# The first chunk of a fused mLSTM and MLP kernel: up-projection blocks in quarters, clearings on ScalarE, a new order of conversions

## The chip, the cores and the metric

The kernel runs on one core of a Trainium2 chip. The metric is device time in microseconds: 498.03 us, the median of 13 runs (496.6 to 499.7). The core has five engines that run their own instruction queues in order and meet at semaphores: TensorE (matrix products, PE in the profile, its weight loads PEld), VectorE (DVE), ScalarE (ACT), GpSimd (POOL) and SyncE (SP), which here issues all DMA transfers.

## The reference

Two stages. The first is an mLSTM cell: for 4 batches x 8 heads, head size 40, over 768 time steps, a matrix memory is decayed, added to and read out.

```python
for t in range(S):
    kt, vt, qt = (k[:, :, t], v[:, :, t], q[:, :, t])
    m_new = np.maximum(f_gate[:, :, t] + m, i_gate[:, :, t])
    f_stab = np.exp(f_gate[:, :, t] + m - m_new)
    i_stab = np.exp(i_gate[:, :, t] - m_new)
    m = m_new
    C = f_stab[:, :, None, None] * C + i_stab[:, :, None, None] * np.einsum('bhd,bhe->bhde', vt, kt)
    n = f_stab[:, :, None] * n + i_stab[:, :, None] * kt
    h_tilde = np.einsum('bhde,bhe->bhd', C, qt)
    nq = np.einsum('bhd,bhd->bh', n, qt)[:, :, None]
    denom = np.maximum(np.abs(nq), 1.0)
    o = 1.0 / (1.0 + np.exp(-o_gate[:, :, t]))
    y[:, :, t] = o * h_tilde / denom
```

Its output, as 3072 tokens x 320, feeds the second stage, with w_in 320 x 2048 and w_out 2048 x 320. All arrays but the two weight matrices are float32; those two are float64.

```python
h = x @ w_in
g = h * (1.0 / (1.0 + np.exp(-1.702 * h)))
return (g @ w_out).astype(np.float32)
```

## The kernel before

**Chunks.** The 768 steps are cut into six chunks of 128 (`w` = 0 to 5). A chunk's attention is computed as within-chunk products plus what the carried state gives. Each chunk then goes through the MLP: an up part of eight blocks `j` with two output tiles of 128 hidden units x 512 tokens (4 batches x 128), and a down part in which the attention of the next chunk is interleaved. The order of all instructions is written out by hand: each engine runs its share in program order.

**The attention steps of chunk 0**, one batch `b` at a time:

- `transposes(0, b)` (L297) transposes keys and queries by TensorE and copies them out of PSUM by ScalarE (L310).
- `weights(0, b)` (L319) builds the exponents of the decay weights by small bf16 products (L324, L328, L329) from `pick`, `m3` and `a3`, in two halves, and ScalarE takes their exponential (L330). `m3` comes from VectorE and `a3` from GpSimd, both in `gates(0)` (L239), which starts with a scan over the gates (L244).
- `scores(0, b)` (L341) multiplies keys and queries; VectorE multiplies the result into the weights (L349).
- `values(0, b)` (L351) multiplies weights and values; VectorE divides and applies the output gate (L383 to L389), and GpSimd copies 64 columns of y (L391). With `states=True` it also emits `scale_values` (L402), in which GpSimd multiplies the values by their decay for the state.
- `seam(0, b)` (L393) transposes y by TensorE into `p_x`, and ScalarE copies it to `xT` (L399), the input of the MLP.
- `gate_out(b)` (L684) is ScalarE's tanh of the output gate. `columns(0)` (L283) brings per-step factors into columns.

**PSUM.** There are three rings of banks: `ps_a` with four tiles, used in turn by every attention step (a new tile waits until the readers of the tile four places before it are done), `ps_m` with two and `ps_x` with two, which hold the up blocks' sums. `keep_busy(n)` (L183) issues `n` bf16 products of zeros (128 x 512); nobody reads them. Before the change they all go to one tile of `ps_m`.

**Weights.** A float64 weight is loaded as two 32-bit words and turned into a float32 by `convert(n)` (L222), in pieces of 128 x 512: two ScalarE instructions ("A", L227 and L228) and then four VectorE ones ("V", L231 to L236). Pieces 0, 1, 3, 4, 5, 6, 8 and 9 are rows 0 to 255 of w_in: blocks 0 and 1 need pieces 0 and 1, blocks 2 and 3 need 3 and 4, blocks 4 and 5 need 5 and 6, blocks 6 and 7 need 8 and 9. Pieces 2 and 7 hold rows 256 to 319, for blocks 0 to 3 and 4 to 7. Pieces 10 to 19 are w_out. `fetch(n)` (L156) issues a piece's loads on SP, into a slot that an earlier piece must have left.

**The up part of chunk 0.** `up(w, j, n)` (L447) computes `n` blocks. A block is `full` (two 128-row parts of w_in, for both tiles) and `rest` (the last 64 rows), then the GELU by ScalarE (L474). For blocks 0 and 1, `full` is done for the first 256 tokens (batches 0 and 1), then a function `between` is called, then the other 256 tokens follow. That function is `rest_of_first` (L732): values, seams and conversions of batches 2 and 3. `weights_in(n)` (L744) calls `convert` and then `fetch` for the pieces in a table: `weights_in(0)` converts piece 5 and fetches 10 to 15.

**Clearings.** Early in the kernel, GpSimd clears the padding of the key and query buffers, `k_bl` (128 x 2048, L203) and, later, `state` (128 x 1312, L710).

The calls that set the order of chunk 0, from L700 to L730, and the functions that the diff touches:

Of the kernel before, what the change touches and what calls it, by code (L numbers as in the profile page):

```python
# [8 lines left out]
FP = mybir.dt.float32  # L9
U32 = mybir.dt.uint32  # L10
BF = mybir.dt.bfloat16
AF = mybir.ActivationFunctionType
# [10 lines left out]
L = 128  # L23
# [11 lines left out]
def kernel(  # L35
# [22 lines left out]
    W = B * L  # L58
# [118 lines left out]


    idle = const.tile([128, 128], BF, name="idle")
    V.memset(idle, 0.0)  # L180
    p_idle = ps_m.tile([128, W], FP, tag="m", name="p_idle")

    def keep_busy(n):  # L183
        for _ in range(n):
            T.matmul(p_idle, idle, idle.unsqueeze(1).to_broadcast([128, 4, 128]), start=True, stop=True)

    keep_busy(8)
    ident = const.tile([128, 128], FP, name="ident")
    make_identity(nc, ident)
    one1 = const.tile([BH, 1], FP, name="one1")  # L190
# [9 lines left out]
    for t in (k_st, q_st):  # L200
        G.memset(t[:, :, D:DP], 0.0)
    G.memset(v_st[:, :, D:D1], 1.0)
    G.memset(k_bl, 0.0)  # L203

    not_yet, ident_bf = (xs.bitcast(BF)[:, i * L:(i + 1) * L] for i in range(2))
    V.memset(not_yet, 0.0)
    G.affine_select(out=not_yet, in_=not_yet, compare_op=OP.is_ge, fill=NEG, base=0, pattern=[[1, L]],
                    channel_multiplier=-1)
    V.tensor_copy(out=ident_bf, in_=ident)
# [1 line left out]
    a3 = const.tile([3 * BH, L], BF, name="a3")  # L211
    m3 = const.tile([3 * BH, L], BF, name="m3")
    state = const.tile([128, BH // 2, 2, D1], FP, name="state")

    t1, t2, t4 = (const.tile([128, NH, DH], FP, name=f"t{i}") for i in (1, 2, 4))

# [124 lines left out]
    def scores(w, b):  # L341
        pool, tag = (ps_x, "x") if w > 1 and b % 2 == 0 else (ps_a, "a")
        pw = [pool.tile([L, NP, L], FP, tag=tag, name="p_s") for _ in range(2)]
        for p in range(NP):
            for i in range(2):
                r = slice(i * 64, i * 64 + D)
                T.matmul(pw[i][:, p, :], kT[w, b][r, p, :], qT[w, b][r, p, :], start=True, stop=True)
        for i in range(2):
            V.tensor_tensor(out=wt[w, b][:, :, i, :], in0=pw[i], in1=wt[w, b][:, :, i, :], op=OP.mult)  # L349
# [43 lines left out]
    def seam(w, b):  # L393
        if b == 0:
            xT[w] = work.tile([128, 3, B, L], FP, tag="xT", bufs=1, name="xT")
        px = ps_a.tile([128, 3, L], FP, tag="a", name="p_x")
        for c in range(3):
            T.transpose(px[:, c, :], ys[w, b][:, c * 128:(c + 1) * 128], ident)  # L398
        A.copy(out=xT[w][:, :, b, :], in_=px)  # L399
# [44 lines left out]

    w_half = [[w_in_sb[:, c, :].rearrange("p (n h m) -> h p n m", h=2, m=256)[i] for c in range(2)] for i in range(2)]

    def up(w, j, n, between=None, states=False):  # L447

        x = xT[w].rearrange("p c b t -> p c (b t)")
        begin, end = range(j, j + n // 2), range(j + n // 2, j + n)
        ph = {}

        def take(j, pool, tag):
            ph[j] = [pool.tile([128, W], FP, tag=tag, name="p_h") for _ in range(2)]

        def full(j, first, ts=slice(0, W)):
            for c in range(2):  # L460
                for i in range(2):
                    T.matmul(ph[j][i][:, ts], w_half[i][c][:, j // 2, j % 2 * 128:(j % 2 + 1) * 128], x[:, c, ts],  # L462
                             start=(first and c == 0 and ts.start == 0), stop=(not first and c == 1),
                             skip_group_check=between is not None)

        def rest(j, first):
            for i in range(2):
                r = slice(i * 64, i * 64 + 64)
                T.matmul(ph[j][i], w_in_x[r, j, :], x[r, 2, :], start=first, stop=not first,
                         skip_group_check=between is not None)  # L470

        def gelu(j):
            for i, g in enumerate(hidden_of(w, j)):
                A.activation(out=g, in_=ph[j][i], func=AF.Gelu_apprx_sigmoid)  # L474

        if between:
            begin, end = (j, j + 1), ()
        for k in begin:
            take(k, *((ps_m, "m") if k == j else (ps_x, "x")))
            full(k, True, slice(0, W // 2 if between else W))  # L480
        if between:
            between()
            for k in begin:
                full(k, True, slice(W // 2, W))
        if states:
            new_states(w)
            carry(w)
        for k in begin:
            rest(k, False)
            gelu(k)  # L490
        for k in end:
            if k not in ph:
                take(k, *((ps_x, "x") if n == 2 else (ps_a, "a")))
            rest(k, True)
        for k in end:
            full(k, False)
            gelu(k)
# [209 lines left out]
    gate_out(0)  # L707
    gate_out(1)
    values(0, 0)
    G.memset(state, 0.0)  # L710
    convert(0, "A")
    values(0, 1)
    keep_busy(2)
    seam(0, 0)
    transposes(0, 2)
    convert(0, "V")
    seam(0, 1)
    convert(1, "A")
    weights(0, 2)
    keep_busy(2)  # L720
    transposes(0, 3)
    weights(0, 3)
    convert(1, "V")
    columns(0)
# [2 lines left out]
    scale(0, 0)  # L727
    scale(0, 1)
    scores(0, 2)
    scores(0, 3)  # L730

    def rest_of_first():  # L732
        values(0, 2, 3, states=True)
        seam(0, 2)
        seam(0, 3)
        for n in (2, 3, 4):
            convert(n)

# [15 lines left out]
    for w in range(NW):  # L756
        more = w + 1 < NW
        for j in range(NF // 2):
            if j % 2 == 0:
                if w:  # L760
                    if j % 4 == 0:
                        if w > 1:
                            up_fast(w, j, next_keys if more and j == 0 else None)
                        else:
                            up(w, j, 4, states=(j == 0))
                elif j == 0:
                    up(w, j, 2, rest_of_first)
                    weights_in(0)
                else:
                    weights_in(j // 2)  # L770
                    up(w, j, 2, states=(j == 2))
            if j == 0 and more:
                load(w + 1, "o")
            if w == 0 and j == 0:
                load_blocks(1, 0)
                spread(1)
            if w == 1 and j == 1:
                weight_sums()
                first_sums()
            if more:  # L780
                if w == 1 and j == 0:
                    gates(w + 1)
                if j == 4:
                    if w == 0:
                        load_blocks(1, 1)
                    load(w + 1, "v")
                    if w:
                        spread(w + 1)
                if j == (4 if w else 6):
                    load(w + 1, "k")  # L790
                if w == 1 and 4 <= j < 6:
                    transposes(w + 1, 2 * j - 8)
                    transposes(w + 1, 2 * j - 7)
            if w > 1 and more and j == 3:
                transposes(w + 1, 2)
                transposes(w + 1, 3)
            if w and j in (3, 7):
                hidden_sums(w, 0, (j // 4 * 2, j // 4 * 2 + 1), 1, 2)
                if j == 3:
                    hidden_sums(w, 0, (0, 1), 3, 4)  # L800
        side = attention(w + 1) if more else []
        if w == 0:

            blocks = [(lambda b=b, n=n: down(w, b, n)) for ns in ((0, 1), (2,), (3,)) for b in range(B) for n in ns]
            stops = (0, 1, 5, 7, 9, 11, 13, 15)
        else:
            blocks = down_fast(w, 0) + down_fast(w, 1)
            stops = (0, 1, 2, 4, 8, 10, 11, 12)
        for i, block in enumerate(blocks):
            if w == 0:  # L810
                weights_in(4 + i)
                for b in {2: (0, 1), 7: (2,), 9: (3,)}.get(i, ()):
                    transposes(1, b)
            elif w + 2 < NW and i == 0:
                load_gates(w + 2)
                load_blocks(w + 2)
            block()
            if i in stops and side:
                run(side.pop(0))
            if w:  # L820
                for at, c, *what in ((0, 0, (2, 3), 3), (1, 0, (2, 3), 4), (1, 1, range(4), 1),
                                     (5, 1, range(2), 2), (6, 1, range(2, 4), 2), (7, 1, range(4), 4)):
                    if i == at:
                        hidden_sums(w, c, *what)
                if i == 2 and not more:
                    hidden_sums(w, 1, range(4), 3)
            if w == 1 and i == 9:
                first_difference()
        if w == 0:
            load_gates(2)  # L830
            load_blocks(2)
# [30 lines left out]
```

## Time and profile before

| | us |
|---|---|
| median of 13 runs | 498.03 |
| lowest and highest run | 496.6, 499.7 |
| the profiled execution | 496.6 |
| its span, first to last instruction | 494.9 |
| TensorE busy | 484.4 |
| VectorE busy | 330.7 |
| ScalarE busy | 207.3 |
| GpSimd busy | 63.1 |

The profile describes one execution. Its page gives the busy time of each engine, then the span in 40 equal slices of 12.4 us, each digit the busy share in tenths, and the clock granted to TensorE in tenths of full speed. Queries of the same trace give the list of waits (who waited for whom), the timeline (start and length of instructions, merged where alike, with the idle time before them in brackets and what ended it), and busy times in chosen stretches. A float32 product appears as two instructions for one matmul of the program. DMA issues have a time from issue to landing. A matmul's end is modelled, so products that follow each other closely overlap in the rows.

### The profile page before, as it was taken

What the parts mean: (1) busy time and instruction counts of PE and PEld (TensorE: products, weight loads), DVE (VectorE), ACT (ScalarE), POOL (GpSimd) and SP (SyncE); (2) the same over time, 40 slices, a digit from 0 to 9 for tenths busy, and PEclk for the clock granted to TensorE, in tenths of its full rate; (3) what the DMA queues carried; (4) which work ended last, traced back from release to release, by engine and by line L of the source; (5) the groups of instructions that cost most, each with busy time, mean ns of one, the idle gap of its engine ahead of it and who ended that gap; (6) DMA issues with size and microseconds to landing.
All of it is one profiled execution on the core that took longest, in us unless ns stands there. A gap on an engine that the chain in (4) does not pass through costs nothing. (4 is left out here: it accounts for less than half of the span.)

```text
span 494.9 us, 10268 instructions
## 1 busy us (share of the span) xinstructions
PE 484.4 (98%) x4028; PEld 388.2 (78%) x4028; DVE 330.7 (67%) x819; ACT 207.3 (42%) x533; POOL 63.1 (13%) x105
## 2 busy tenths in 40 slices
PE   7979999999999999999999999999999999999997
PEld 4765447776446999877999977999977999877897
DVE  8758975893693787586686676786666776344841
ACT  3728569121223800374900364920255940155400
POOL 5120001231000322000232000142000030000000
PEclk9999999999999999999999999999999999999999
DMA  9998899502699620597300398400195000000000
GB/s 133 186 273 285 130 280 146 77 1 69 71 153 228 74 42 1 100 252 83 35 28 3 71 263 85 50 16 15 34 267 59 2 1 28 28 0 3 0 28 26
DMA packets 175952, 44.85 MB, mean 91 GB/s; under 512 B 164352, under 2 KB 169504, under 8 KB 175904
## 3 DMA queue, kind: packets, MB, share of 16 engines
q1 hardware_dynamic: 175904, 44.21, 47.9%
q8 instruction: 31, 0.51, 0.4%
q14 instruction: 17, 0.14, 0.1%
HBM read 40.17 MB, written 4.01 MB: 89 GB/s over the span
## 5 line engine op out<-in xcount | busy, mean ns | idle before, releaser
L399 ACT COPY xT<-p_x 128x384 f32<-128x384 f32 x24 | 11.1, 480 | 140.6 <-PE p_x L398 140.6
L633 PE MATMUL p_out<-w_out_sb,g 128*128 128x160 f32 x480 | 69.8, 301 | 0.0
L633 PEld LDWEIGHTS p_out<-w_out_sb,g 128*128 128x128 f32 x480 | 66.4, 190 | 1.4 <-issue 0.5
L462 PE MATMUL p_h<-xT,w_in_sb 128*128 128x512 f32 (+1 forms) x144 | 59.1, 565 | 1.1 <-ACT xT L399 1.1
L542 DVE TENSOR_TENSOR g<-p_u,g 128x256 f32<-128x256 f32 x64 | 27.2, 425 | 40.8 <-PE p_u L534 32.8
L462 PEld LDWEIGHTS p_h<-xT,w_in_sb 128*128 128x128 f32 x144 | 27.8, 198 | 30.9 <-issue 26.8
L336 POOL TENSOR_SCALAR_AFFINE_SELECT wt<-wt 128x1024 f32<-128x1024 f32 x20 | 22.4, 1120 | 226.8 <-ACT wt L334 226.8
L539 ACT COPY g<-p_u 128x256 f32<-128x256 f32 x96 | 34.4, 377 | 34.5 <-PE p_u L534 31.2
L638 DVE TENSOR_TENSOR o_sb<-o_sb,p_out 128x160 f32<-128x160 f32 x70 | 21.3, 317 | 41.2 <-PE p_out L633 40.9
L334 ACT ACTIVATE wt<-wt,cols 128x128 f32<-128x128 f32 x160 | 48.0, 395 | 0.0
L546 ACT ACTIVATE g<-g 128x256 f32<-128x256 f32 x96 | 33.9, 425 | 31.3 <-DVE g L542 31.3
L349 DVE TENSOR_TENSOR wt<-p_s,wt 128x512 f32<-128x512 f32 x48 | 30.4, 682 | 11.6 <-POOL wt L336 6.3
L582 PE MATMUL p_out<-w_out_sb,g 128*128 128x320 f32 x128 | 36.2, 437 | 0.0
L633 PE MATMUL p_out<-t,big 128*128 128x160 f32 x240 | 35.5, 301 | 0.0
L474 ACT ACTIVATE g<-p_h 128x512 f32<-128x512 f32 x32 | 17.8, 599 | 38.8 <-PE p_h L462 20.0
L633 PEld LDWEIGHTS p_out<-t,big 128*128 128x128 f32 x240 | 33.3, 190 | 0.2
L582 PEld LDWEIGHTS p_out<-w_out_sb,g 128*128 128x128 f32 x128 | 23.8, 190 | 10.1 <-issue 0.5
L534 PE MATMUL p_u<-xT,w_in_sb 128*128 128x256 f32 x128 | 31.2, 382 | 0.0
L534 PE MATMUL p_u<-xs,big 128*128 128x256 f32 x128 | 30.3, 379 | 0.0
L562 PE MATMUL p_v<-xT,w_in_x 64*128 64x512 f32 x64 | 29.6, 602 | 0.0
L562 PE MATMUL p_u<-xT,w_in_x 64*128 64x512 f32 x64 | 29.6, 602 | 0.0
L534 PEld LDWEIGHTS p_u<-xT,w_in_sb 128*128 128x128 f32 x128 | 23.7, 190 | 4.5 <-DVE o_sb L638 1.5
(160 smaller groups left out, 851.3 us busy)
## 6 DMA issues: line engine op xcount, KB each, us to landing
wt<-m_row SPq DMA_DIRECT2D x20, 512.0 KB, 6.2
out_dram<-o_sb SPq DMA_DIRECT2D x24, 160.0 KB, 1.8
eo<-in_o_gate_dram SPq DMA_DIRECT2D x5, 640.0 KB, 5.6
v_st<-in_v_dram SPq DMA_DIRECT2D x5, 640.0 KB, 8.8
k_st<-in_k_dram SPq DMA_DIRECT2D x5, 640.0 KB, 11.1
big<-in_moe_w_in_dram SPq DMA_DIRECT2D x5, 512.0 KB, 6.7
big<-in_moe_w_out_dram SPq DMA_DIRECT2D x8, 320.0 KB, 4.4
k_bl<-in_k_dram SPq DMA_DIRECT2D x40, 64.0 KB, 2.7
```

The lines of the kernel that those rows point to most:

```text
L334: A.activation(out=x[:, h, :], in_=x[:, h, :], func=AF.Exp, scale=-1.0, bias=cols[w][:, b * H + h:b * H + h + 1])
L336: G.affine_select(out=x, in_=x, compare_op=OP.is_ge, fill=0.0, base=0, pattern=[[0, H], [1, L]], channel_multiplier=-1)
L349: V.tensor_tensor(out=wt[w, b][:, :, i, :], in0=pw[i], in1=wt[w, b][:, :, i, :], op=OP.mult)
L462: T.matmul(ph[j][i][:, ts], w_half[i][c][:, j // 2, j % 2 * 128:(j % 2 + 1) * 128], x[:, c, ts], start=(first and c == 0 and ts.start == 0 ...
L534: T.matmul(p[k][:, ts[t]], a[:, k // 2, k % 2 * 128:(k % 2 + 1) * 128], b, start=first, stop=True, skip_group_check=True)
L539: A.copy(out=g[k][i][:, ts[t]], in_=chain[k][:, ts[0]])
L542: V.tensor_tensor(out=g[k][i][:, ts[t]], in0=p[k][:, ts[pt]], in1=g[k][i][:, ts[t]], op=OP.add)
L546: A.activation(out=dst, in_=dst if src is None else src, func=AF.Gelu_apprx_sigmoid)
L562: T.matmul(p[k], w_in_x[r, k, :], x[r, 2, :], start=False, stop=True, skip_group_check=True)
L582: T.matmul(po, gs[w, f // 2][:, f % 2, b * L:(b + 1) * L], w_out_sb[:, f, :], start=(f == 0), stop=(f == NF - 1))
L633: T.matmul(po, a(f), b[:, f, :], start=(f == 0), stop=(f == NH - 1))
L638: V.tensor_tensor(out=dst, in0=x, in1=po, op=OP.add)
```

## The change

- A tile of `ps_a` is now taken by each call of `keep_busy` (the first eight products stay in `ps_m`). There are new calls: one of 2 between `seam(0, 0)` and `seam(0, 1)` instead of the one behind `weights(0, 2)`, one of 2 between `seam(0, 2)` and `seam(0, 3)`, one of 3 after `seam(0, 3)`.
- `k_bl` and `state` are cleared by ScalarE at the start, as copies of a zero, instead of by GpSimd. VectorE's clearing of `not_yet` moves to the front of its queue.
- `transposes(0, 2)` and `weights(0, 2)` move ahead of `seam(0, 0)`; `transposes(0, 3)` moves behind `scores(0, 2)`. ScalarE's part of convert(1) thereby stands ahead of the exponentials of `weights(0, 3)` instead of those of `weights(0, 2)`.
- The first 256 tokens of blocks 0 and 1 are now four separate pieces of two products (`full_rows(j, c, 0)`, one for each block and each 128-row part), placed between the attention steps of batches 2 and 3. `values(0, 2)` and `values(0, 3)` become two calls.
- ScalarE's part of convert(2) moves ahead of the seams of batches 2 and 3. `weights_in(0)`, with convert(5) and the fetches of pieces 10 to 15, moves ahead of the GELUs of blocks 0 and 1.

The diff, without the parts that only take the parameter `between` out of `up`:

```diff
@@ -177,14 +177,17 @@
     idle = const.tile([128, 128], BF, name="idle")
+    not_yet, ident_bf = (xs.bitcast(BF)[:, i * L:(i + 1) * L] for i in range(2))
     V.memset(idle, 0.0)
-    p_idle = ps_m.tile([128, W], FP, tag="m", name="p_idle")
-    def keep_busy(n):
+    V.memset(not_yet, 0.0)
+    def keep_busy(n, pool=ps_a, tag="a"):
+        p_idle = pool.tile([128, W], FP, tag=tag, name="p_idle")
         for _ in range(n):
             T.matmul(p_idle, idle, idle.unsqueeze(1).to_broadcast([128, 4, 128]), start=True, stop=True)
-    keep_busy(8)
+    keep_busy(8, ps_m, "m")
     ident = const.tile([128, 128], FP, name="ident")
     make_identity(nc, ident)
     one1 = const.tile([BH, 1], FP, name="one1")
@@ -200,10 +203,6 @@
     for t in (k_st, q_st):
         G.memset(t[:, :, D:DP], 0.0)
     G.memset(v_st[:, :, D:D1], 1.0)
-    G.memset(k_bl, 0.0)
-    not_yet, ident_bf = (xs.bitcast(BF)[:, i * L:(i + 1) * L] for i in range(2))
-    V.memset(not_yet, 0.0)
     G.affine_select(out=not_yet, in_=not_yet, compare_op=OP.is_ge, fill=NEG, base=0, pattern=[[1, L]],
                     channel_multiplier=-1)
     V.tensor_copy(out=ident_bf, in_=ident)
@@ -211,6 +210,8 @@
     a3 = const.tile([3 * BH, L], BF, name="a3")
     m3 = const.tile([3 * BH, L], BF, name="m3")
     state = const.tile([128, BH // 2, 2, D1], FP, name="state")
+    for t in (k_bl.rearrange("p j g c -> p (j g c)"), state.rearrange("p j a b -> p (j a b)")):
+        A.copy(out=t, in_=idle[:, 0:1].to_broadcast(t.shape))
     t1, t2, t4 = (const.tile([128, NH, DH], FP, name=f"t{i}") for i in (1, 2, 4))
...
@@ -707,18 +698,16 @@
     gate_out(0)
     gate_out(1)
     values(0, 0)
-    G.memset(state, 0.0)
     convert(0, "A")
     values(0, 1)
     keep_busy(2)
+    transposes(0, 2)
+    weights(0, 2)
     seam(0, 0)
-    transposes(0, 2)
+    keep_busy(2)
+    seam(0, 1)
     convert(0, "V")
-    seam(0, 1)
     convert(1, "A")
-    weights(0, 2)
-    keep_busy(2)
-    transposes(0, 3)
     weights(0, 3)
     convert(1, "V")
     columns(0)
@@ -727,14 +716,40 @@
     scale(0, 0)
     scale(0, 1)
     scores(0, 2)
+    first = [[pool.tile([128, W], FP, tag=tag, name="p_h") for _ in range(2)] for pool, tag in ((ps_m, "m"), (ps_x, "x"))]
+    x_first = xT[0].rearrange("p c b t -> p c (b t)")
+    def full_rows(j, c, t):
+        ts = slice(t * (W // 2), (t + 1) * (W // 2))
+        for i in range(2):
+            T.matmul(first[j][i][:, ts], w_half[i][c][:, 0, j * 128:(j + 1) * 128], x_first[:, c, ts],
+                     start=(c == 0 and t == 0), stop=True, skip_group_check=True)
+    full_rows(0, 0, 0)
+    transposes(0, 3)
+    full_rows(1, 0, 0)
     scores(0, 3)
-    def rest_of_first():
-        values(0, 2, 3, states=True)
-        seam(0, 2)
-        seam(0, 3)
-        for n in (2, 3, 4):
-            convert(n)
+    values(0, 2, states=True)
+    full_rows(0, 1, 0)
+    convert(2, "A")
+    values(0, 3, states=True)
+    full_rows(1, 1, 0)
+    seam(0, 2)
+    keep_busy(2)
+    seam(0, 3)
+    keep_busy(3)
+    convert(2, "V")
+    convert(3)
+    convert(4)
+    for j in range(2):
+        for c in range(2):
+            full_rows(j, c, 1)
+    for j in range(2):
+        for i in range(2):
+            r = slice(i * 64, i * 64 + 64)
+            T.matmul(first[j][i], w_in_x[r, j, :], x_first[r, 2, :], start=False, stop=True, skip_group_check=True)
@@ -764,8 +779,10 @@
                         else:
                             up(w, j, 4, states=(j == 0))
                 elif j == 0:
-                    up(w, j, 2, rest_of_first)
                     weights_in(0)
+                    for pair_ in range(2):
+                        for i, g in enumerate(hidden_of(0, pair_)):
+                            A.activation(out=g, in_=first[pair_][i], func=AF.Gelu_apprx_sigmoid)
                 else:
                     weights_in(j // 2)
                     up(w, j, 2, states=(j == 2))
```

More of the change, by code (lines that the diff above doesn't have):

```diff
@@ L445, with up @@
     w_half = [[w_in_sb[:, c, :].rearrange("p (n h m) -> h p n m", h=2, m=256)[i] for c in range(2)] for i in range(2)]
-    def up(w, j, n, between=None, states=False):
+    def up(w, j, n, states=False):
         x = xT[w].rearrange("p c b t -> p c (b t)")
@@ L457, in take, with full @@
             ph[j] = [pool.tile([128, W], FP, tag=tag, name="p_h") for _ in range(2)]
-        def full(j, first, ts=slice(0, W)):
+        def full(j, first):
             for c in range(2):
                 for i in range(2):
-                    T.matmul(ph[j][i][:, ts], w_half[i][c][:, j // 2, j % 2 * 128:(j % 2 + 1) * 128], x[:, c, ts],
-                             start=(first and c == 0 and ts.start == 0), stop=(not first and c == 1),
-                             skip_group_check=between is not None)
+                    T.matmul(ph[j][i], w_half[i][c][:, j // 2, j % 2 * 128:(j % 2 + 1) * 128], x[:, c, :],
+                             start=(first and c == 0), stop=(not first and c == 1))
         def rest(j, first):
@@ L468, in rest @@
                 r = slice(i * 64, i * 64 + 64)
-                T.matmul(ph[j][i], w_in_x[r, j, :], x[r, 2, :], start=first, stop=not first,
-                         skip_group_check=between is not None)
+                T.matmul(ph[j][i], w_in_x[r, j, :], x[r, 2, :], start=first, stop=not first)
         def gelu(j):
@@ L474, in gelu @@
                 A.activation(out=g, in_=ph[j][i], func=AF.Gelu_apprx_sigmoid)
-        if between:
-            begin, end = (j, j + 1), ()
         for k in begin:
             take(k, *((ps_m, "m") if k == j else (ps_x, "x")))
[L480 to L484, printed above, removed]
+            full(k, True)
         if states:
```

## Prediction

> **What bounds the kernel now.** I read the page's shares first, then the slices.
>
> ```profile
> PE 484.4 (98%) x4028; PEld 388.2 (78%) x4028; DVE 330.7 (67%) x819; ACT 207.3 (42%) x533; POOL 63.1 (13%) x105
> ...
> PE   7979999999999999999999999999999999999997
> PEclk9999999999999999999999999999999999999999
> ```
>
> TensorE is busy in every slice but the first and the third (0 to 12.4 and 24.7 to 37.1 us). The list of waits, TensorE alone, from 38 us to the end, holds two entries:
>
> ```profile
> PE p_h L462 <- ACT xT L399: 0.6, 1, 0.6
> PE p_out L633 <- DVE o_sb L638: 0.4, 1, 0.4
> ```
>
> So from 38 us on TensorE waits 1.0 us in 457. The changed instructions all lie ahead of about 45 us: what brings that dense stretch forward shows at the end, and what adds TensorE work there delays it. Next the stretches around the third slice (columns: stretch, length, PE busy and instructions, granted clock, DMA share, GB/s):
>
> ```profile
> 32.00:33.00 1.00, 0.00 (x0) 1.00 0.97 320
> ...
> 35.00:36.00 1.00, 0.43 (x3) 0.99 1.02 209
> 36.00:37.00 1.00, 1.00 (x3) 0.50 1.08 248
> ...
> 38.00:39.00 1.00, 1.00 (x4) 0.50 1.07 395
> 39.00:40.00 1.00, 1.00 (x6) 0.81 1.04 384
> ```
>
> After a stretch with almost no products (31.9 to 35.8) the clock is 0.50 for about 3.4 us. The timeline names the chain that ends the idle stretch (start, length, engine, line):
>
> ```profile
> 34.05 0.49 DVE L389 SCALAR_TENSOR_TENSOR y<-eo,den 128x320 f32<-128x320 f32 x1
> 34.60 0.24 POOL L391 COPY y<-y 128x64 f32<-128x64 f32 x1 [1.23 <-DVE y L389]
> ...
> 35.26 0.48 ACT L399 COPY xT<-p_x 128x384 f32<-128x384 f32 x1 [0.98 <-PE p_x L398]
> ...
> 35.79 5.41 PE L462 MATMUL p_h<-xT,w_in_sb 128*128 128x256 f32 x16 [0.57 <-ACT xT L399]
> ```
>
> The same 16 quarter instructions took 3.72 us at 26.19 (timeline); here 5.41. The first slices:
>
> ```profile
> 1.40 3.37 DVE L198 TENSOR_SCALAR pick<-ident 32x32 bf16<-32x32 f32 x3 [0.40 <-POOL ident masks.py:199]
> ...
> 2.73 1.83 POOL L203 MEMSET k_bl<- 128x2048 f32 x1
> ...
> 4.94 0.40 DVE L244 TENSOR_TENSOR_SCAN f_run<-one,fi 32x128 f32<-32x128 f32 x1
> ...
> 9.28 0.23 PE L329 MATMUL p_w<-pick,a 96*128 96x128 bf16 x1 [0.43 <-POOL a L253]
> ```
>
> Three tiny `pick` writes last 0.17, 1.35 and 1.82 us, the long ones ending with GpSimd's clearings; the gate scan, and by GpSimd's `a3` the first weights, wait behind them.
>
> **Part 1: the start.** GpSimd loses the 1.83 us clearing of k_bl and that of state (1.19 at 18.10). VectorE then does the second and third `pick` in 0.17 each after 2.75, the cast in 0.16, and can scan at about 3.5 instead of 4.94 (gates issued at 0.81 and 1.26, 1.7 to land: 3.0). `a3` moves from 9.22 to about 7.8, the first exponentials from 9.88 to 8.4. The next link is later than that: the second chunk's gates land at 8.8 and 9.1 (issues at 4.52 and 5.70, 4.3 and 3.4 to land), so its gate work, 2.41 us ahead of the first score multiplication, ends at 11.3 instead of 12.51. The multiplication, the second batch's scores (ring of four PSUM tiles) and values(0,1) follow: 15.35 instead of 16.45. Here the gain is 1.1.
>
> Clearing by ScalarE has no row. Nearest: 128x1280 tanh, 1.29 us; at 0.83 ns an element 2048 cost 1.93 and 1312 cost 1.32, 3.25 together. They start at 2.08 behind the table load and end near 5.3; the first key copy comes at 5.88. So nothing; at twice the price they end at 8.6, and this gain, no more, is gone.
>
> **Part 2: 15.35 to scores(0,2).** TensorE, in its new order: dummies 0.43, transposes(0,2) 0.9 (its keys and queries land at 15.9 and 16.45), weights(0,2) 1.3, seam 0.35, dummies 0.43, seam 0.35, weights(0,3) 1.3, columns 0.25, with values(0,1) 1.05 ahead of it: 6.4, to 21.75. The dummies now take places in the ring. So scores(0,2) needs the place of weights(0,3)'s first half, whose exponential stands in ScalarE's queue behind convert(1,"A") (1.25 us, from 20.8; its piece landed at 19.4): 22.6, scores at 22.75. A new wait of 1.0 for TensorE; behind it is everything, so the gain is 24.03-22.75 = 1.28, and I take 1.2.
>
> **Part 3: scores(0,2) (time S) to the second halves.** Scores 1.1, quarter 0.9, transposes(0,3) 0.9, quarter 0.9, a wait for the copies of about 0.1, scores 1.1, values(0,2) 1.05, quarter 0.9, values(0,3) 1.05: S+8.0. The last quarter runs beside VectorE. values(0,2)'s VectorE work (1.54 a batch) is done by then, which it was not before (31.02 to 33.08, with one write at 1.00 instead of 0.49 beside GpSimd's multiplication). So y(3) is at S+9.7, and the old 1.25 from y to the first product gives S+10.95, against 35.79-24.03 = 11.76: 0.8. Hand-overs that do not fit so well could take all of it, and a second slow y 0.5; I take 0.5. The batch 3 gate lands at 25.0, its tanh ends at 25.45 and the key copy behind it is due at 25.45: no slack, no loss. convert(2,"A"), now ahead of the seam copies, waits for piece 2 until 27.8 and ends at 29; the copies are due after 31.
>
> **Part 4: the clock.** With the dummies, the worst 3.4 us (about 31 to 34) hold some 0.5 of quarter, 1.1 of dummies and 0.7 of transposes, 65%; before, 0.2 of products and 0.7 of transposes. The row so far: clock 0.50 after 26%. A rule speaks against me: the Trainium skill, TensorE: Matmul & The Clock Gate, Part 4, says transposes do not count as busy for the clock. Then it is 47% against 5%. The stretch 5.3 to 8.7, by this count about 19% with two dummies in it, was followed by products 55 ns apart at 9.3, at speed; so I take the full clock and 5.41-3.7 = 1.7. If the rule and a stricter limit held, this would be 0.
>
> The five added dummies (11 against 6 behind the first eight, 0.215 each, 1.1) cost nothing: two wait in the 1 us between seam(0,2) and y(3), three in the 0.8 of the last copy.
>
> **Part 5: ScalarE ahead of the GELUs.** convert(5) moves ahead of them. Behind the last seam copy (about 33.9) stand convert(3), (4), (5), 3.45 together, and the table load: the first GELU can start at 38.6. It was 1.16 behind the start of `rest`, which comes at 33.95+3.7 = 37.65: due 38.8. For the load I take 1.28:
>
> ```profile
> 74.05 0.19 ACT L291 COPY cols<-p_cols 128x32 f32<-128x32 f32 x1 [0.67 <-PE p_cols L289]
> 74.25 1.28 ACT L292 ACT_TABLE_LOAD   x1
> ...
> 75.54 0.22 ACT L292 ACTIVATE cols<-p_cols 128x64 f32<-128x64 f32 x1
> ```
>
> Copy to exponential is 1.30 here. The skill's ScalarE: Activation LUTs, What ACT_TABLE_LOAD costs, puts 1.38 of drain on top: 40.0, and 1.2 of wait for TensorE's next block (it needs the GELUs' PSUM). The row decides; I charge 0.1. Piece 5 landed at 33.1, 3 us early. VectorE's conversions (2.45 a piece, back to back from 32.6): piece 2 at 35, 3 at 37.5, 4 at 39.9; needed at 37.7, 39.6 and 41.3.
>
> SP: fetch(10) to (15) keep their place ahead of the next chunk's loads; SP waited 3.3 us there for the conversion of piece 5, now some 4 us earlier (42.3 against 47.3), so the later loads move with TensorE. Without that the cover is thin: the query transpose at 81.49 waited 1.99 for its load, 2.6 ahead of scores at 84.80.
>
> **Sum.** 1.2+0.5+1.7-0.1 = 3.3. The profiled execution took 496.6 (span 494.9): 493.3. It is the lowest of 13 runs; the median lies 1.43 higher, and 498.03-3.3 = 494.7.
>
> **Rivals.** (a) 0.57: as summed, 493.6 to 496.0 (each part at its ends, without losing one altogether). (b) 0.22: one of the large parts is missing. The clock still drops: 498.03-1.6 = 496.4; or the start stays bound by transfers and ScalarE's wait takes the rest: 498.03-2.1 = 495.9. For: DMA share is above 0.9 in 20 of the first 26 us. Against: only the first keys and queries, landing at 5.0 and 6.3, are waited for. (c) 0.11: both are missing, or the change doesn't do what it says because a transfer (the gate at 25.0) holds values(0,3): gain 0 to 1, 497.6. (d) 0.10, slower: ScalarE becomes the bound at the GELUs. Every us that the first starts after 38.8 holds TensorE by one; the sum of 3.3 is used up at 42.1, and over 0.2% is lost from 43.1. It would take piece 5 landing at about 40.5 rather than 33.1, as piece 9 does (40.8): 499.3. Against: the issue order is unchanged.
>
> **Numbers.** The measurement tells 0.2%, 1.0 us. Faster by more: (a), (b) and none of (c): 0.79; within: 0.11; slower: 0.10. The range takes (a), (b) and the better part of (c): below, 493.2, as runs above the lowest may have lost more to the clock; above, 497.5. (a) alone: 493.6 to 496.0.
>
> **What would show it.** Right: the scan at 3.5, scores(0,2) near 22.8, second halves near 34, 3.7 us long at clock 1.00, GELU near 38.8. Wrong: clock 0.50 after 34 (part 4), a scan after 4.5 (part 1), second halves after 35 (2, 3), TensorE waiting for GELU after 39.5 (5), or new TensorE waits around 82 (SP).

## The result

The changed kernel takes 493.1 us (median of 11 runs, 492.83 to 494.76); the kernel before, over all 48 runs made of it by then, 498.05. The ratio is 0.9894, 95% interval [0.9869, 0.9919]. The forecast was 494.7, in a range of 493.2 to 497.5: the direction held, and the kernel is 0.1 faster than the range allowed and 1.6 faster than the forecast. The profiled executions went from 496.6 (span 494.9) to 492.95 (span 491.2), 3.65, close to the summed 3.3; the medians differ by 4.95. Runs of one and the same kernel differ by how many stretches of 3.4 us TensorE spends at clock 0.50: the profiled run of before has one, its median run by its mean clock two, and every run of the changed kernel made here shows a mean clock of 0.999 or 1.000.

The page of the changed kernel, shares and slices:

```profile
PE 484.2 (99%) x4033; PEld 388.0 (79%) x4033; DVE 328.6 (67%) x819; ACT 211.0 (43%) x535; POOL 60.7 (12%) x103
...
PE   8999999999999999999999999999999999999997
```

The third slice, 7 before, is full, and where the clock of before was 0.50 (36.0 to 39.4) it is now 1.00, as it is ahead of the second halves (stretch, length, PE busy and instructions, clock, DMA share, GB/s):

```profile
33.00:34.00 1.00, 1.00 (x6) 1.00 1.13 262
34.00:35.00 1.00, 1.00 (x5) 1.00 0.99 195
```

The list of waits for TensorE alone, from 34 us to the end:

```profile
PE p_h L461 <- ACT xT L400: 0.6, 1, 0.6
PE p_out L624 <- DVE o_sb L629: 0.4, 1, 0.4
```

These are the two waits of before: the dense stretch has been moved whole. The timeline of the start (start, length, engine, line):

```profile
1.40 1.84 DVE L201 TENSOR_SCALAR pick<-ident 32x32 bf16<-32x32 f32 x3 [0.32 <-POOL ident masks.py:199]
...
2.10 1.90 ACT L214 CAST k_bl<-idle 128x2048 f32<-128x2048 bf16 x1
...
3.40 0.40 DVE L245 TENSOR_TENSOR_SCAN f_run<-one,fi 32x128 f32<-32x128 f32 x1
...
7.75 0.23 PE L330 MATMUL p_w<-pick,a 96*128 96x128 bf16 x1 [0.38 <-POOL a L254]
```

The three `pick` writes take 1.84 instead of 3.37, the scan starts at 3.40 instead of 4.94, the first weights at 7.75 instead of 9.28; ScalarE's clearing costs 1.90 and 1.28 in time it had free. The chain that ends at the second halves (VectorE's last y starts at 31.99):

```profile
33.33 0.48 ACT L400 COPY xT<-p_x 128x384 f32<-128x384 f32 x1 [0.55 <-PE p_x L399]
...
33.86 3.72 PE L727 MATMUL p_h<-xT,w_in_sb 128*128 128x256 f32 x16
```

It ends 1.93 earlier (33.86 against 35.79), and the 16 quarter products take 3.72 instead of 5.41. Together that is the 3.6 by which the next block starts earlier (39.43 against 43.05).

### The profile page after: what moved, and what is told of

Its sections match the earlier page's. It is cut to its first block, busy times and chain, and to the rows that moved or that the text cites. A ratio compares the mean times of both kernels' runs of the same rounds, so it can differ in the third digit from the quotient of the medians.

```text
span 491.2 us, 10275 instructions
## 1 busy us (share of the span) xinstructions
PE 484.2 (99%) x4033; PEld 388.0 (79%) x4033; DVE 328.6 (67%) x819; ACT 211.0 (43%) x535; POOL 60.7 (12%) x103
## 5 line engine op out<-in xcount | busy, mean ns | idle before, releaser
L461 PE MATMUL p_h<-xT,w_in_sb 128*128 128x512 f32 x112 | 49.9, 599 | 0.6 <-ACT xT L400 0.6
L461 PEld LDWEIGHTS p_h<-xT,w_in_sb 128*128 128x128 f32 x112 | 20.7, 190 | 28.8 <-issue 26.7
L350 DVE TENSOR_TENSOR wt<-p_s,wt 128x512 f32<-128x512 f32 x48 | 30.5, 682 | 12.7 <-PE p_s L348 6.5
L471 ACT ACTIVATE g<-p_h 128x512 f32<-128x512 f32 x28 | 15.7, 598 | 38.1 <-PE p_h L461 20.0
L573 PEld LDWEIGHTS p_out<-w_out_sb,g 128*128 128x128 f32 x128 | 23.8, 190 | 10.1 <-issue 0.5
L348 PE MATMUL p_s<-qT,kT 40*128 40x128 f32 x384 | 26.3, 281 | 1.0 <-ACT qT L311 0.6
```

The lines of the kernel that those rows point to most:

```text
L461: T.matmul(ph[j][i], w_half[i][c][:, j // 2, j % 2 * 128:(j % 2 + 1) * 128], x[:, c, :], start=(first and c == 0), stop=(not first and c = ...
L573: T.matmul(po, gs[w, f // 2][:, f % 2, b * L:(b + 1) * L], w_out_sb[:, f, :], start=(f == 0), stop=(f == NF - 1))
```

## The experiments

Each kernel was timed beside the kernel before. The mean granted clock of a run counts its lost stretches: 3.4 us at half clock in 495 is 0.0034, so 0.997 is one, 0.993 two, 0.989 or 0.990 three, 0.986 four, 0.983 five. Profiles were taken of runs with none, one and two; from three on the count is this sum alone. Runs by their clock:

| kernel | runs | 1.000 or 0.999 | 0.997 or 0.996 | 0.993 or 0.992 | 0.990 and less | median us |
|---|---|---|---|---|---|---|
| before (beside the first four) | 48 | 0 | 15 | 21 | 12 | 498.02 |
| changed (the result) | 11 | 11 | 0 | 0 | 0 | 493.10 |
| before again | 22 | 0 | 5 | 9 | 8 | 498.16 |
| before + late dummies | 14 | 5 | 2 | 5 | 2 | 497.29 |
| changed, no late dummies | 7 | 6 | 1 | 0 | 0 | 492.97 |
| changed, clearing by GpSimd | 18 | 6 | 7 | 0 | 5 | 495.67 |
| before (beside the next four) | 38 | 0 | 16 | 16 | 6 | 497.60 |
| before + clearing by ScalarE | 22 | 4 | 8 | 10 | 0 | 496.33 |
| before + dummies at both places | 17 | 17 | 0 | 0 | 0 | 495.56 |
| changed, gate later | 5 | 5 | 0 | 0 | 0 | 492.56 |
| changed, gate and convert later | 6 | 6 | 0 | 0 | 0 | 491.74 |
| before (beside the last three) | 27 | 0 | 11 | 10 | 6 | 498.05 |
| changed again | 6 | 5 | 1 | 0 | 0 | 493.06 |
| changed, quarters together | 14 | 1 | 8 | 5 | 0 | 498.06 |
| gate and convert later, loads earlier | 14 | 0 | 1 | 12 | 1 | 499.13 |

### The kernel before, unchanged

> The kernel before, unchanged, to see what its runs above 496.6 us spend their extra time on. Theory (clock): they show a lower mean granted clock and a longer span, by steps of about 1.7 us, because a second stretch of 3.4 us runs at clock 0.50; a profile of such a run shows 0.50 in two places. Rival (outside): span and clock are the same, about 495 us and 0.997, and the extra time lies outside the span or in transfers. Ratio to itself 1.000.

Measured: 498.16, ratio 1.0004 [0.998, 1.0028]. Time follows clock: the spans are 494.7 to 495.0 at 0.997, 495.8 to 496.6 at 0.992 or 0.993, 497.7 to 497.8 at 0.989 and 500.4 to 500.5 at 0.983. The clock theory held, with steps of about 1.3 to 1.5 rather than 1.7. This time the profile caught a run at 0.993. Its stretches (length, PE busy and instructions, clock, DMA share, GB/s):

```profile
34.00:35.00 1.00, 0.17 (x2) 1.00 1.04 184
35.00:36.00 1.00, 0.43 (x4) 0.64 1.03 213
36.00:37.00 1.00, 1.00 (x3) 0.50 1.03 215
...
41.00:42.00 1.00, 1.00 (x3) 0.50 0.74 278
42.00:43.00 1.00, 1.00 (x5) 0.95 0.73 182
```

Here 0.50 holds for 6.8 us in the same place where the first profile has 3.4: two stretches in a row, although TensorE is dense from 35.94 us on. The median run of before has the same mean clock, so two stretches; they need not both be in this place (the next profile, at 0.993 too, has one here and one near 10 us).

### The late dummies alone, and the change without them

```diff
         seam(0, 2)
+        keep_busy_a(2)
         seam(0, 3)
+        keep_busy_a(3)
```

`keep_busy_a` is the change's `keep_busy` with a tile of `ps_a`.

> The kernel before with only the two late groups of dummies of the change (2 behind the seam of batch 2, 3 behind that of batch 3). Clock theory: second halves still start near 35.8 us but take 3.7 instead of 5.4; span 493.2, and the median falls by more than 1.7 (to 495 to 496.3) if the runs above the lowest lose to the clock in the same place. Rival: the dummies alone do not hold the clock; span and median stay at 494.9 and 498.0.

Measured: 497.29, ratio 0.9993 [0.9963, 1.0024]. Neither expectation fits: 5 of 14 runs keep the full clock (spans 493.7 and 493.8), which none of the 135 runs of before in the table does; the others lose one to four stretches. So these dummies help in some runs and don't hold the clock. Its profile, at 0.993, shows 0.50 from 9.3 to 12.7 and from 36.6 to 40.0.

```diff
     seam(0, 2)
-    keep_busy(2)
     seam(0, 3)
-    keep_busy(3)
```

> The changed kernel without those two groups of dummies. Theory that they hold the clock: 0.50 after about 34 us, second halves 5.4 us instead of 3.7, span 492.9, median 1.7 or more above the changed kernel (494.8 and up). Rival that the quarters placed between the attention steps hold it: span 491.2, median 493.1.

Measured: 492.97, ratio 0.9909 [0.9875, 0.9944], beside 493.1 with them. The rival's numbers came: the late dummies are not needed in the new order. TensorE's late pause in this kernel:

```profile
31.00:32.00 1.00, 0.97 (x6) 1.00 1.08 395
32.00:33.00 1.00, 0.67 (x3) 1.00 1.09 285
33.00:34.00 1.00, 0.43 (x2) 1.00 1.02 236
```

With the last quarter behind values(0,3), the pause is some 2 us, not 3.9, and the clock stays at 1.00 without dummies.

### The clearings

```diff
-    for t in (k_bl.rearrange(...), state.rearrange(...)):
-        A.copy(out=t, in_=idle[:, 0:1].to_broadcast(t.shape))
...
+    G.memset(k_bl, 0.0)
...
     values(0, 0)
+    G.memset(state, 0.0)
```

> The changed kernel with both clearings back on GpSimd at their old places. Theory: the gate scan starts near 4.9 us instead of 3.4, values(0,1) near 16.4 instead of 14.9; the second halves start later by what the transfer of batch 3's output gate (landing at 25.0) leaves: scores(0,2) ends about 1.2 later, the key copy waits for the tanh less, so 0.4 to 0.7; span 491.6 to 491.9, median about 493.6. Rival: the whole 1.2 comes through: 492.4 and 494.3.

Measured: 495.67, ratio 0.9969 [0.9942, 0.9995]: 2.6 worse than the changed kernel, beyond both expectations. The runs at 1.000 have spans of 492.1 to 492.8, against 490.8 to 491.4 in most runs of the changed kernel, about the 1.2 of the rival: the order's share. The rest is clock. The profiled run:

```profile
8.00:9.00 1.00, 0.14 (x1) 1.00 1.37 168
9.00:10.00 1.00, 0.57 (x9) 1.00 1.32 182
10.00:11.00 1.00, 1.00 (x11) 0.53 1.35 180
11.00:12.00 1.00, 1.00 (x8) 0.50 1.01 171
```

TensorE waits, for `m3` and then for `a3`, and is nearly idle from 7.5 to 9.5; a stretch at 0.50 follows, to 13.5. The changed kernel is busy there and has no such stretch:

```profile
8.00:9.00 1.00, 1.00 (x17) 1.00 1.40 167
```

The reverse, this part alone, with VectorE's clearing of `not_yet` at the front:

```diff
-    G.memset(k_bl, 0.0)
...
-    G.memset(state, 0.0)
...
+        A.copy(out=t, in_=idle[:, 0:1].to_broadcast(t.shape))
```

> The kernel before with one part of the change: both clearings by ScalarE, and the clearing of the mask ahead. Theory (two idle places, each of which can cost stretches at clock 0.50): the wait for a3 ends at 7.8 instead of 9.2 us, so no 0.50 near 10 to 13 us in any run, but the late gap (32 to 36) stays, so 0.997 and 0.993 remain and the runs at 0.989 and below go; with one stretch 493.9 (1.1 of start) in the span. Median 496 to 496.5. Rival (all of the loss is late): the same steps of clock as before, down to 0.983, median 496.9.

Measured: 496.33 beside 497.6 for the 38 runs of before, ratio 0.996 [0.9941, 0.998]; profiled span 494.0 at 0.997, with the one stretch from 34.7 to 38.1. As expected, no run lies below 0.992, and 18 of 22 runs keep one or two stretches. Not expected: 4 runs keep the full clock, although the order behind the start, with its late gap, is that of before.

### The clock without the order

```diff
     transposes(0, 0)
+    keep_busy(8)
     weights(0, 0)
...
         values(0, 2, 3, states=True)
+        keep_busy_a(6)
         seam(0, 2)
+        keep_busy_a(4)
         seam(0, 3)
+        keep_busy_a(3)
```

> The kernel before, its order unchanged, with dummies in both idle places: 8 ahead of the first weights, 6, 4 and 3 around the late seams. Theory: granted clock 1.000 in all runs, span 493.2 (the profiled 494.9 less one stretch of 1.7), median 494.9, all runs within 0.5: then the clock is 3.1 of the 4.95 us by which the medians differ, and the order 1.8. Rival: other places lose clock too, or the dummies delay TensorE: clock below 1.000 or median above 496.

Measured: 495.56 (495.33 to 495.6), ratio 0.9944 [0.992, 0.9968], span 493.6 to 493.8, clock 1.000 or 0.999 in all 17 runs. The second halves start at 35.78, against 35.79 in the profile of before, so the dummies delay nothing there. Then 498.05-495.56 = 2.49 of the change's 4.95 is clock and 495.56-493.1 = 2.46 is order. (Against the 38 runs timed beside this kernel, 497.60, the clock's share is 2.04; the order's doesn't depend on that sample.) The expected 494.9 is missed by 0.66. Part of that is visible, in the block behind the second halves:

```profile
41.35 1.98 PE L467 MATMUL p_h<-xT,w_in_sb 128*128 128x512 f32 x4
43.54 1.98 PE L467 MATMUL p_h<-xT,w_in_sb 128*128 128x512 f32 x4 [0.20 <-DVE w_in_sb L241]
45.45 1.43 PE L429 MATMUL p_c<-v_st,k_st 128*40 128x41 f32 x64
```

At full clock the old order runs into VectorE's conversion of piece 4. From this block's start to `p_c` it takes 4.10 us, in the changed kernel (39.43 to 43.06) 3.63. The order's share is thus 1.92 for the block's start and 0.47 for the conversions: 2.4.

### What bound the new order

```diff
     gate_out(2)
-    gate_out(3)
...
     transposes(0, 3)
+    gate_out(3)
     full_rows(1, 0, 0)
```

> The changed kernel with the tanh of batch 3's output gate behind the key and query copies of that batch instead of ahead of them. Theory (the transfer of that gate, landing at 25.0, holds the copies and with them scores(0,3), TensorE idle 0.62 to 0.8 there): second halves at 33.2 instead of 33.86, span 490.6, median 492.5. Rival: values(0,3) or the conversions bind next, span 491.2.

The changed kernel at this place (timeline):

```profile
25.05 0.47 ACT L677 ACTIVATE eo<-eo 128x320 f32<-128x320 f32 x1 [1.33 <-DMA eo<-in_o_gate_dram]
25.42 0.57 ACT L311 COPY kT<-p_t 128x512 f32<-128x512 f32 x1
25.89 0.59 ACT L311 COPY qT<-p_t 128x512 f32<-128x512 f32 x1
...
26.53 1.16 PE L348 MATMUL p_s<-qT,kT 40*128 40x128 f32 x16 [0.62 <-ACT qT L311]
```

Measured: 492.56, ratio 0.9866 [0.981, 0.9923]; second halves at 33.20, span 490.6 or 490.7 in four of five runs: the theory's numbers. The profiled run, at a span of 491.3, waits 0.7 near 81 us for a query transpose. The second step:

```diff
     convert(0, "V")
-    convert(1, "A")
     weights(0, 3)
-    convert(1, "V")
     columns(0)
+    convert(1, "A")
     gate_out(2)
...
     scores(0, 2)
+    convert(1, "V")
```

> As the one before, and ScalarE's part of convert(1) behind the exponentials of weights(0,3) and the columns, VectorE's part behind the first multiplication of scores(0,2). Theory: TensorE's wait of 0.5 ahead of scores(0,2) for ScalarE goes too; second halves at 32.7, span 490.1, median 492.0. Rival: VectorE, which now converts piece 1 between the multiplications, delays values(0,3), or GELUs bind on ScalarE: span 490.6 or more.

Measured: 491.74, ratio 0.986 [0.9813, 0.9906]; second halves at 32.63; four of six runs have spans of 489.7 to 489.9 (490.1 was expected), two 491.4 and 491.5. It has the lowest median of all, 1.3 under that of the changed kernel, which was timed at another time. Its list of waits for TensorE, in the profiled run, one of the longer ones:

```profile
PE p_s L348 <- DVE qT L302: 1.5, 1, 1.5
```

That is where the next bound lies: VectorE's transpose of the second chunk's queries waited 5.42 us for their load to land.

### The quarters in one group, and earlier loads

```diff
-    full_rows(0, 0, 0)
     transposes(0, 3)
-    full_rows(1, 0, 0)
     scores(0, 3)
+    full_rows(0, 0, 0)
+    full_rows(0, 1, 0)
+    full_rows(1, 0, 0)
+    full_rows(1, 1, 0)
     values(0, 2, states=True)
-    full_rows(0, 1, 0)
...
     values(0, 3, states=True)
-    full_rows(1, 1, 0)
```

> The changed kernel again, beside the next two on the same chip: span 491.0 to 491.5 in most runs, granted clock 1.000, median 493.1.

> The changed kernel with the four quarters in one group behind scores(0,3), as before, the two values calls behind them; the late dummies stay. Theory (the quarters between the attention steps close the late gap): TensorE idle again for 2 us or more ahead of the second halves, these start near 34.8 instead of 33.86, and part of the runs show 0.997 or less; median 494.2 or more. Rival (the start and the dummies hold the clock): clock 1.000 in all runs, span later by the 0.9 us of the moved quarter only, median 494.0.

The changed kernel again: 493.06, ratio 0.9896 [0.9855, 0.9937], spans 490.8 to 491.4 in five of six runs, as expected. With the quarters together: 498.06, ratio 0.9998 [0.9972, 1.0025], the whole gain lost, 5.0 where 1.1 was expected. The profiled run (0.993):

```profile
26.36 2.08 PE L348 MATMUL p_s<-qT,kT 40*128 40x128 f32 x16 [2.23 <-ACT qT L311]
28.37 5.97 PE L727 MATMUL p_h<-xT,w_in_sb 128*128 128x256 f32 x16
```

The first two quarters had covered the wait for batch 3's gate; without them TensorE idles from about 24.1 to 26.4, and the clock is 0.50 for 6.8 us (two stretches), from 26.1 to 33. So the test shows what the quarters are worth in their places, but it moved the loss to a new place and doesn't isolate the late gap. In the one run at 1.000 the span is 494.1.

```diff
         for p in ahead:
+            if p == 12:
+                load_blocks(1, 0)
             fetch(p)
...
-                load_blocks(1, 0)
                 spread(1)
+                load_blocks(1, 1)
```

> The kernel with the later gate and the later convert(1), and with the next chunk's key blocks issued ahead of the fetch of piece 12 and its query blocks right behind the spread of the stabilizer rows. Theory (where that kernel shows TensorE waiting for a query transpose near 81 us, the cause is the place of those loads in SP's queue): no such wait, span 489.7 in all runs, median 491.5. Rival: the key loads delay pieces 8 and 9 or 12 to 15, and TensorE waits between 55 and 75 us: span above 490.5.

Measured: 499.13, ratio 1.0011 [0.9987, 1.0036]: refuted. The list of waits:

```profile
PE p_s L348 <- DVE qT L302: 3.6, 1, 3.6
```

The wait grew from 1.5 to 3.6 (79.9 to 83.6 us), and the clock is 0.50 for two stretches (82.2 to 89.0). The key blocks' issues took 10.3 us instead of 14.7, but the issues of the spread took 7.8 instead of 2.2, and the query blocks left SP by 75.1, 3.5 earlier only. But this time the queries are not what is waited for. The edit puts the query blocks ahead of the fetches of pieces 16 and 17 as well, whose issues thereby start at 75.2 instead of 63.5. ScalarE waits 8.24 us for the first of the two (to 79.15), VectorE 9.50 for ScalarE, and VectorE's conversion of it, to 82.3, stands ahead of the transposes that TensorE needs. So the earlier loads displaced weights, as the rival said; it was the query loads that did it, to later pieces than the rival named. Why the spread's issues are slower is not shown.

## Why the prediction was wrong in size

**The bound and its place: right.** TensorE's dense stretch moved as a whole.

**Part 1: right in the order, too small in its clock.** Scan 3.40 (3.5 said, although one of the three `pick` writes still takes 1.35 rather than 0.17), first weights 7.75 (`a3` at 7.8), values(0,1) at 14.93 (15.35). Its worth of 1.1 to 1.2 is about what the runs at full clock show: 1.2 between the changed kernel with GpSimd's and with ScalarE's clearings, and 0.9 to 1.0 in the old order (492.6 to 492.9 against 493.6 to 493.8). But the wait that it shortens, some 2 us near 8, is itself a place where the clock is lost: both profiles with 0.50 from 9.3 or 10.1 on have it just before. I had not read it so, because the profile given had no 0.50 there.

**Parts 2 and 3: the sum right, its terms not.** I had S at 22.75 and 10.95 behind it. TensorE started scores(0,2) at 21.12, stopped after one product for ScalarE's exponential and went on at 21.95; the second halves came 11.9 after that, against 11.76 before and 10.95 summed, so part 3 gave nothing. What failed is "no slack, no loss": once S is 0.8 earlier than summed, the gate's landing at 25.0 is a loss, and moving the tanh gives 0.66 back. Together 1.93 against 1.7.

**Part 4: the size right for one stretch, the cause not, the count not.** 3.72 against 5.41 is the 1.7 as said. The dummies I gave as the reason are not needed (nothing is lost without them); what is different from before is a pause of some 2 us instead of 3.9, with products in it. Which of the moved pieces does that was not isolated: the test that put the quarters together lost its clock elsewhere, so that the last quarter does it is argued, not shown. The busy share with dummies adds to 68% (2.3 of 3.4), not 65%; nothing hangs on it. No run tells whether transposes count for the clock.

**The failed step** is the one behind the sum: "The profiled execution took 496.6 ... the median lies 1.43 higher, and 498.03-3.3 = 494.7." I took the 1.43 as an offset that any kernel keeps. It is a second stretch at 0.50, of the kind that the change removes: the changed kernel's median lies 0.15 above its profiled run. That is 1.28 of the 1.6 by which the forecast missed; the rest is that the sum itself fell 0.35 short (3.3 against 3.65). By term, at the median, the clock measures 2.49 (1.7 summed) and the order 2.46 (1.6 summed); 0.47 of the latter, the conversions that no longer hold the next block, was not in the sum at all. The range's reason, "runs above the lowest may have lost more to the clock", named it, and gave it 1.5 us below the forecast where 1.6 were needed. That the median fell outside the range by 0.1 is within the spread of the runs (492.83 to 494.76); the missing term is not.

**Part 5: right.** The chain on ScalarE:

```profile
37.26 1.28 ACT L785 ACT_TABLE_LOAD   x1
...
38.67 2.07 ACT L785 ACTIVATE g<-p_h 128x512 f32<-128x512 f32 x4
```

38.67 (38.6 to 38.8 said), 1.16 behind the start of `rest` and 0.13 behind the load: the 1.38 of drain that the Trainium skill, ScalarE: Activation LUTs, What ACT_TABLE_LOAD costs, puts on top is not there. VectorE's conversion of piece 5 moves by the 5.0 of its two numbers (42.3 against 47.3), not by "some 4"; it ended at 41.9. The thin cover at the query transpose was real: the changed kernel doesn't touch it, the next two do.

**Open:** the four stretches (0.986) in 5 of 18 runs with GpSimd's clearing were not profiled, nor any run of before at 0.989 or less; that the early place is part of them follows only from their absence once ScalarE clears. Why one run loses one stretch and the next two is not shown. One hint stands in the profile with two separate stretches (before + late dummies): they begin 27.3 us apart, 8 times 3.41. Whether stretches begin only at such steps, so that one and the same pause is caught in one run and missed in another, was not tested.

## What to carry over

When the runs of a kernel fall into steps, read the granted clock of each run before adding a saving to the median: the profile shows one of the steps, and a change that closes TensorE's pauses removes the steps as well. Dummies can hold the clock if there are enough: 8 in the early pause and 13 in the late one did in 17 of 17 runs, 5 in the late one alone in 5 of 14. Real work moved into the pauses needed none of the late ones and brought the start of the next block forward as well. A pause that ends earlier exposes the transfer that landed in its shadow.

## What the runs showed of the hardware

One kernel lost, by its mean clock, from one to five stretches of 3.4 us at half clock in different runs, 494.7 to 500.5 us of span in the 22 runs of before again, with nothing changed. A pause of about 2 us near 8 us cost the clock in one run and not in another: TensorE was 0.55, 0.14 and 0.57 busy in three neighbouring microseconds of a run that lost it (changed, clearing by GpSimd), and 0.21, 0.21 and 0.57 in one that did not (before again). The clock fell to 0.50 2.0 us after the last product in one pause (24.1 to 26.1, quarters together) and 2.2 in another (79.9 to 82.2, loads earlier), while TensorE still stood idle. A stretch at 0.50 could be followed directly by a second although TensorE was dense for most of the first (before again: 0.50 from 35.3 to 42.1, dense from 35.94). ScalarE copied a zero into 128x2048 in 1.90 us and into 128x1312 in 1.28.
